# Side sums on the tiles of the main loop: attention and a long convolution on one core

## The chip, the cores and the metric

The kernel runs on one core of a Trainium2 chip. The metric is the device time of one execution in microseconds, and the change is judged by the ratio of the times after and before. TensorE (PE) multiplies matrices into PSUM, which has eight banks of 512 fp32 columns on 128 partitions. ScalarE (ACT) computes the exponentials, VectorE (DVE) everything elementwise; SyncE (SP), ScalarE and GpSimd (POOL) have queues that issue DMAs. Each engine works off its own instructions in order and waits for the others at semaphores.

## The reference

Two independent heads over 2048 positions and 576 channels, concatenated. Everything is fp32.

```python
# A: a diagonal state-space layer, as a long convolution; D = 576 channels, N = 128 states
P = jnp.exp(logdA[:, :, None] * l[None, None, :])           # l = 0..2047
K = jnp.einsum("dn,dnl,dn->dl", Cc, P, dB).real             # one kernel of 2048 taps per channel
y = irfft(rfft(u padded to 4096) * rfft(K padded))[:, :2048] + u * Dskip
# B: attention with 32 query heads of 18 and one head of keys and values
q = (x @ wq).reshape(B, S, 32, 18); k = x @ wk; v = x @ wv  # k, v: 2048 x 18
p = softmax(q k^T * 18 ** -0.5); out = (p v) @ wo
return concatenate([a, b], axis=-1)
```

## The kernel before

**The main loop** is the attention. A *score* is one pair of heads against 128 keys for 512 queries: eight matmuls, each on a tile of 64 rows by 32 columns of the array, fp16, into a two-bank PSUM tile `s` (two such tiles take turns). ScalarE takes the exponential of the whole tile, 128 x 1024, into `P` (ten buffers). A *product* (`ops`) multiplies the exponentials of two scores with the values, fp32, again eight matmuls on 64x32 tiles: the upper 64 rows accumulate into one bank, the lower 64 into another, and VectorE adds the two banks at the end of a group of 16 key blocks (`gather`). A group is four heads, a chunk (`c`) is 512 queries: 4 chunks x 8 groups x 16 key blocks x 2 = 1024 scores and 512 products.

**The side sums** are all other matmuls, put between scores and products: the query projection `q` (five k-steps, two column halves; 4 chunks x 5 units `m`), the output projection `op` (five k-steps, two halves of 288 columns, four row blocks a chunk; the last chunk's in parts as its heads finish), and the convolution, which runs in 12 chunks of 48 channels: `kg` multiplies out the convolution kernel from tables of powers, `hu`, `lu`, `hk`, `lk` are the cosine and sine transforms of the input `u` and of the kernel `kt`, `iy` the inverse. Each is made by

```python
def matmul4(nc, ps, w, x, start=True, stop=True):
    for j in range(0, n, 32):
        nc.tensor.matmul(ps[j:e], w[:, j:e], x, start=start, stop=stop, tile_position=(0, j))
```

or the like: four matmuls on tiles of 128 rows by 32 columns. Attention's side sums and the convolution's have one PSUM bank each (`ps_f["a"]`, `ps_f["c"]`). VectorE empties a bank (`evacuate`, `tensor_copy` and so on) before the next sum goes into it.

**The order** of the three engines PE, ACT and DVE is written out when the program is built. `main` keeps a clock of its own for each engine, with a price for each kind of work, and decides what TensorE does next: a score, a product, or a step of a side sum. Generators wrapped in `Stream` stand for the attention's side work (`side`), its normalisation (`prep`) and two streams of the convolution (`fronts` builds tables and kernel, `backs` transforms and multiplies); they say "p" when they want TensorE, "v" for VectorE. In the clock a change between 64-row and 128-row tiles costs `SWITCH`, so side steps are bunched by `ENTER`, `STAY` and `DRY` in `choose`. `RATE` says how much VectorE work of the convolution may be issued per pair of scores.

**The end.** The kernel `ksb` of a convolution chunk goes through memory to change its layout: `kg`, evacuation, DMA `kd`, four DMAs `kt`, then `hk`/`lk`, some 30 elementwise products and sums (`ks`, `acc`, `sv`, `w`), `iy`, the addition to `u`, and the DMA `outa`. When the scores are done, `drain` finishes the convolution and `finish` the output projection of the last chunk.

Of the kernel before, what the change touches and what calls it, by code (L numbers as in the profile page):

```python
# [47 lines left out]
RATE = 1.9  # L48
# [6 lines left out]
DRY = 1.0  # L55
ENTER = 0.7
EDGE = 0.25
STAY = 0.4
# [18 lines left out]
class Clock:  # L77


    def __init__(self):  # L80
        self.t = self.v = self.a = 0.0
        self.work = self.side = 0.0
        self.last = ""
        self.tiling = 0
        self.s = [0.0] * NS
        self.fill = {"a": 0.0, "c": 0.0}

    def tile(self, rows):

        if rows != self.tiling:  # L90
            self.tiling, self.t = rows, self.t + SWITCH

    def pe(self, cost, *after):
        self.tile(128)
        self.t = max(self.t, *after) + cost if after else self.t + cost
        self.side += cost

    def main(self, cost, *after):
        self.tile(64)
        self.t = max(self.t, *after) + cost  # L100
# [5 lines left out]
    def filled(self, bank):  # L106

        self.fill[bank] = self.v + 0.25
# [45 lines left out]
class Stream:  # L154


    def __init__(self, gen, clock, bank, ahead=AHEAD):
        self.gen, self.k, self.bank, self.ahead = gen, clock, bank, ahead
        self.kind, self.ready, self.holds = "v", 0.0, False
        self.live, self.asked, self.work = True, -1, 0.0  # L160

    def advance(self):
        w0 = self.k.work
        r = next(self.gen, None)
        self.work += self.k.work - w0
        if r is None:
# [4 lines left out]
    def at(self):  # L171

        if not self.live or self.kind != "p":
            return 1e9
        return self.ready if self.holds else max(self.ready, self.k.fill[self.bank])

    def event(self):

        if not self.live or self.kind in "wbp":
# [3 lines left out]
    def go(self, step):  # L183

        k = self.k
        if not self.live or self.kind in "bp":
# [11 lines left out]
def matmul4(nc, ps, w, x, start=True, stop=True):  # L198

    n = w.shape[-1]  # L200
    for j in range(0, n, 32):
        e = min(n, j + 32)
        nc.tensor.matmul(ps[j:e], w[:, j:e], x, start=start, stop=stop, tile_position=(0, j))  # L203


class Attention:
# [7 lines left out]
    def __init__(self, tc, ctx, aps, clock):  # L214
# [11 lines left out]
        self.ps_f = {b: pool(f"ps_f{b}", 1, space=PSUM) for b in "ac"}  # L226
# [4 lines left out]
    def bank(self, n, name, bank="a"):  # L231
        self.k.pe(0.0, self.k.fill[bank])
        return self.ps_f[bank].tile([P, CT], F32, tag="f" + bank, name=name)[:, :n]

    def load_x(self, c, pool, **k):
        t = pool.tile([P, 5, CT], F32, name=f"x{c}", **k)
        self.nc.sync.dma_start(t, self.a["xT"][c])
        return t

    def load_wq(self, m):  # L240
        self.nc.sync.dma_start(self.wq[m], self.a["wq"][m, :, :, :MQ[m][1]])

    def setup(self, tp, conv):
# [24 lines left out]
        nc.gpsimd.memset(x0[64:, 4, :], 0.0)  # L268
# [6 lines left out]
        for k in range(5):  # L275
            n = DT[k][1]
            nc.sync.dma_start(x0[:n, k, :], a["xT"][0, :n, k, :])
        nc.scalar.dma_start(self.sel, a["sel"][:, 0:45])
# [1313 lines left out]
```

## Time and profile before

| | |
|---|---|
| median of 3 runs (lowest, highest) | 1172.84 us (1171.32, 1174.79) |
| the profiled execution | 1173.67 us |
| its span, first to last instruction | 1171.9 us |
| busy: PE, ACT, DVE | 1107.6, 1040.0, 1015.0 us |
| mean granted clock of TensorE | 0.991 |

In the rows a group of instructions has the line of the kernel, the engine, the operation and the tiles it writes and reads; `x` is how many. For matmuls "64*32" is the part of the array. An fp32 matmul leaves two records, since it makes two passes, an fp16 one leaves one. A record of a matmul lasts until its modelled end, so back-to-back matmuls overlap: how long TensorE needs for one is seen from start to start. PEld is the weight load, which runs beside the matmuls. "Idle before, releaser" says how long the engine idled before instructions of the group and what ended it.

### The profile page before, as it was taken

Reading aid. Unit: us, or ns where it says so; the run is one execution under the profiler, and the core shown is the slowest. Engines: PE = TensorE matmul, PEld = TensorE weight load, DVE = VectorE, ACT = ScalarE, POOL = GpSimd, SP = SyncE. Lnnn points to the kernel's source line nnn. Section 1 sums busy time; section 2 is a strip of 40 time slices with the busy share of each in tenths; the row PEclk is TensorE's granted clock in tenths of the full one; section 3 lists DMA queues with packets and bytes.
Section 4 is the critical chain, followed back from the end, with each engine's and each line's share of the span. In section 5 each row is a group of like instructions: output and inputs, shape, how many; then the busy total and the mean of one; then the engine's idle time right before and its main releaser. Section 6 shows DMA issues by size and latency. Waiting matters only on the chain.

```text
span 1171.9 us, 53466 instructions
## 1 busy us (share of the span) xinstructions
PE 1107.6 (95%) x24126; PEld 419.0 (36%) x24126; DVE 1015.0 (87%) x1713; ACT 1040.0 (89%) x1052; POOL 141.6 (12%) x257
## 2 busy tenths in 40 slices
PE   6899999999999999999899999999988999999986
PEld 2333333333333333433333333333333333333323
DVE  4868998998998997998899897998789899799583
ACT  3789999998999998999899999888899999999980
POOL 5303310112210100010401100001120000000000
PEclk9999999999999999999999999999999999999998
DMA  7412512113222003131412202113222210302101
GB/s 222 132 49 80 175 29 83 47 44 103 88 69 96 28 32 97 62 112 29 131 47 89 75 25 75 57 40 82 69 68 74 66 36 22 103 30 76 59 21 65
DMA packets 59358, 84.66 MB, mean 72 GB/s; under 512 B 14867, under 2 KB 35335, under 8 KB 58613
## 3 DMA queue, kind: packets, MB, share of 16 engines
q1 hardware_dynamic: 47557, 73.24, 19.5%
q0 software_dynamic: 10848, 7.37, 2.5%
q8 instruction: 190, 3.11, 1.1%
q10 hardware_dynamic: 720, 0.58, 0.2%
q14 instruction: 43, 0.35, 0.1%
HBM read 46.59 MB, written 33.85 MB: 69 GB/s over the span
## 4 chain that ended last, share of the span: by engine, by line
PE 66%; ACT 19%; DVE 7%; issue 4%; DMA 3%; SPq 0%; ACTq 0%; DVEq 0%
PE ops L836 24%; ACT P L538 18%; PE s L527 17%; PE q L418 6%; PE op L203 5%; PE iy L203 3%; PE kg L1260 3%; PE lk L203 2%; PE hk L203 1%; PE lu L203 1%; PE hu L203 1%; DMA xr<-xT 1%; ACT P L536 1%; PE fin L203 1%; DVE t L128 1%
## 5 line engine op out<-in xcount | busy, mean ns | idle before, releaser
L538 ACT ACTIVATE P<-s 128x1024 f32<-128x1024 f32 x992 | 975.8, 1028 | 69.3 <-PE ops L836 17.8
L836 PE MATMUL ops<-P,v_sb 64*32 64x512 f32 x8192 | 539.2, 593 | 1.9 <-DVE u L1050 1.4
L527 PE MATMUL s<-aug,kaug 55*32 55x512 f16 x8192 | 417.6, 383 | 33.1 <-ACT P L538 28.0
L527 PEld LDWEIGHTS <-kaug 55*32 55x32 f16 x8192 | 134.9, 90 | 386.8 <-issue 375.9
L836 PEld LDWEIGHTS ops<-P,v_sb 64*32 64x32 f32 x8192 | 146.9, 106 | 75.8 <-issue 46.0
L468 POOL DMA_DIRECT2D qd<-qh x116 | 66.2, 578 | 412.9 <-DVE qh L136 410.0
L418 PE MATMUL q<-x,wq_sb 128*32 128x256 f32 x1360 | 104.1, 389 | 0.4 <-DVE un L144 0.4
L203 PE MATMUL op<-wo_sb,oT 126*32 126x288 f32 (+1 forms) x1056 | 88.2, 416 | 0.0
L128 DVE TENSOR_TENSOR tab<-tab,tt 128x576 f32<-128x576 f32 (+1 forms) x72 | 59.2, 822 | 2.0
L128 DVE TENSOR_TENSOR tab<-fr,dif 128x576 f32<-128x576 f32 (+1 forms) x72 | 58.7, 815 | 0.0
L128 DVE TENSOR_TENSOR tt<-fr,sum 128x576 f32<-128x576 f32 (+1 forms) x72 | 58.7, 815 | 0.0
L128 DVE TENSOR_TENSOR tab<-sum,fr 128x576 f32<-128x576 f32 (+1 forms) x72 | 58.7, 815 | 0.0
L128 DVE TENSOR_TENSOR tab<-tab 128x576 f32<-128x576 f32 (+1 forms) x72 | 58.6, 814 | 0.0
L418 PEld LDWEIGHTS q<-x,wq_sb 128*32 128x32 f32 x1360 | 29.4, 108 | 71.5 <-issue 64.2
L1171 POOL MEMSET fr<- 128x192 f32 x24 | 9.9, 495 | 371.5 <-DVE tt L128 239.4
L203 PE MATMUL iy<-w,dft_sb 128*32 128x192 f32 x768 | 41.6, 340 | 8.6 <-DVE u L128 8.6
L128 DVE TENSOR_TENSOR acc<-acc,pt 128x1728 f32<-128x1728 f32 (+2 forms) x36 | 48.7, 1354 | 0.7
L128 DVE TENSOR_TENSOR pt<-us,ks 128x1728 f32<-128x1728 f32 (+2 forms) x36 | 48.0, 1351 | 0.3
L536 ACT ACTIVATE P<-s,bias 128x1024 f32<-128x1024 f32 x32 | 32.9, 1124 | 16.6 <-PE s L527 10.6
L132 DVE COPY ksb<-kg 128x192 f32<-128x192 f32 x48 | 17.3, 360 | 33.3 <-PE kg L1260 33.0
L203 PEld LDWEIGHTS op<-wo_sb,oT 126*32 126x32 f32 (+1 forms) x1056 | 22.9, 108 | 60.7 <-issue 50.7
L1260 PEld LDWEIGHTS kg<-tab 128*32 128x32 f32 x2304 | 35.0, 110 | 25.0 <-issue 14.6
(167 smaller groups left out, 1039.5 us busy)
## 6 DMA issues: line engine op xcount, KB each, us to landing
od<-o SPq DMA_DIRECT2D x31, 256.0 KB
aug<-qd SPq DMA_DIRECT2D x124, 55.0 KB
u<-u SPq DMA_DIRECT2D x12, 384.0 KB
kd<-ksb SPq DMA_DIRECT2D x12, 384.0 KB
kt<-kd SPq DMA_DIRECT2D x48, 96.0 KB
outa<-u SPq DMA_DIRECT2D x12, 384.0 KB
pw<-pw SPq DMA_DIRECT2D x8, 528.0 KB
oT<-od SPq DMA_DIRECT2D x16, 252.0 KB
```

The source lines that it names most:

```text
L128: return self.v.tensor_tensor(out, *a, **k)
L132: return self.v.tensor_copy(out, *a, **k)
L203: nc.tensor.matmul(ps[j:e], w[:, j:e], x, start=start, stop=stop, tile_position=(0, j))
L418: nc.tensor.matmul(ps[o, 256 * f:256 * f + 256], w[:, k, i], xt[:, k, x], start=(k == 0), stop=(k == 4), tile_position=(0, 32 * j))
L468: q.dma_start(qd[h:h + n, row + d:row + d + nd, cs], src[i1:i1 + n * nd, :cs.stop - cs.start])
L527: nc.tensor.matmul(ps[e:e + 32, j, :], self.kaug[r, kb * P + e:kb * P + e + 32], t[r, :], start=True, stop=True, tile_position=(64 * j, e))
L536: nc.scalar.activation(pt, ps, AF.Exp, bias=self.bias, scale=SCALE / QQ)
L538: nc.scalar.activation(pt, ps, AF.Exp, scale=SCALE / QQ)
L836: nc.tensor.matmul(o_ps[32 * j:32 * j + 32, b, cs], self.v[r, kb, :], pts[2 * pi + j // 2][r, j % 2, cs], start=(kb == 0), stop=(kb == 15) ...
L1171: nc.gpsimd.memset(t[:, :, 0:NF:8], one)
L1260: nc.tensor.matmul(ps[32 * g:32 * g + 32, d, :], t[:, :32], t[:, 32:], start=(j == 0), stop=(j == 1), tile_position=(0, 32 * g))
```

## The change

All side sums of the loop but three small ones go over to tiles of 64 rows by 32 columns. A sum now has a pair of banks, one for each half of its columns. In the first pass the upper 64 rows of the contraction work for bank 0 and the lower 64 for bank 1; in the second pass they change places. Between the passes stands a drain of TensorE.

```diff
+def halves(nc, ps, cols, w, x, swap, start, stop):
+    for j in range(0, P, 32):
+        for b in range(2):
+            r, i = slice(64 * b, 64 * b + 64), b ^ swap
+            nc.tensor.matmul(ps[j:j + 32, i, cols], w(r, i, j), x(r, i, j), start=start, stop=stop, tile_position=(64 * b, j))
...
-        self.ps_f = {b: pool(f"ps_f{b}", 1, space=PSUM) for b in "ac"}
+        self.ps_f = pool("ps_f", 1, space=PSUM)
...
+    def pair(self, n, name):
+        self.k.pe(0.0, self.k.fill)
+        t = self.ps_f.tile([P, 2, CT], F32, tag="f", name=name)
+        return t[:, :, :n]
+    def flush(self):
+        self.nc.tensor.drain()
+        self.k.pe(0.12)
```

The query projection, whose last k-step has 64 rows of data (laid into both row halves now, by extra loads of x and wq), takes nine steps; the output projection of the first three chunks likewise, with 20 rows a head in a padded layout `wop` of wo (18 rows, two repeated in the other half), for which `normalize` loads the heads with eight DMAs and scales all with one tile of reciprocals. The last chunk loads wo again in the layout of before.

```diff
+        for swap, k in [(0, k) for k in range(5)] + [(1, k) for k in range(4)]:
...
+            if (swap, k) == (1, 0):
+                self.flush()
+            halves(nc, ps, slice(0, n), wi, xi, swap, (swap, k) == (0, 0), (swap, k) == (1, 3))
+            K.pe(0.43 * n / 256)
```

In the convolution `hu` and `lu` become one sum `dtu` in one bank pair (`hk`, `lk`: `dtk`), and the two sums of a `kg` and of an `iy` become one each:

```diff
+            yield "p", max(ready, K.fill), False
+            ps = self.at.pair(2 * NE, f"dt{nm}{j}")
+            for swap, h in ((0, 0), (0, 1), (1, 0), (1, 1)):
+                if (swap, h) == (1, 0):
+                    self.at.flush()
+                halves(nc, ps, slice(h * NE, h * NE + NE), ..., swap, (swap, h) == (0, 0), (swap, h) == (1, 1))
+                K.pe(0.33)
...
+            V.tensor_copy(x, ps[:, :, NE:])
```

Only one side sum is open at a time now (`holder`). The rules that order the work change with it:

```diff
-RATE = 1.9
+RATE = 2.5
...
-DRY = 1.0
-ENTER = 0.7
-EDGE = 0.25
-STAY = 0.4
+DRY = 0.6
+EDGE = 0.3
+URGE = 1.0
+OVER = 0.5
...
-    def tile(self, rows):
-        if rows != self.tiling:
-            self.tiling, self.t = rows, self.t + SWITCH
...
+            if wanted(st) and K.t + 0.45 <= last + (URGE if st is not side and K.v < K.t + DRY else OVER):
                 conv.count(st)
```

What this makes of the order, on TensorE at the first sum of the output projection, first before (`s` is a score, `ops` a product, `op` a step of the sum; a score is eight pairs of LDWEIGHTS and MATMUL):

```order
L836 MATMUL ops_2_7549<-P_5_9_7811,v_sb 32x512 x4
...
L527 MATMUL s_4_11_7864<-aug_113,kaug 32x512
L203 MATMUL op_0_0_7877<-wo_sb,oT_6125 32x288 x4
L527 LDWEIGHTS kaug
...
L836 MATMUL ops_2_7549<-P_5_10_7854,v_sb 32x512 x4
```

and after, where the step has eight matmuls and steps and products stand in no fixed turn:

```order
L878 MATMUL ops_1_7793<-P_3_5_7976,v_sb 32x512 x4
...
L549 MATMUL s_2_7_8074<-aug_113,kaug 32x512
L204 MATMUL op_0_8085<-wo_sb,oT_7064 32x288 x8
L549 LDWEIGHTS kaug
...
L204 MATMUL op_0_8085<-wo_sb,oT_7064 32x288 x16
```

Between two scores now stand one step or two, where before one step was set between two scores and a product between the next two.

TensorE at the end of the loop, before (`iy` is the last chunk's inverse transform, `fin` the closing output sums):

```order
L836 MATMUL ops_7_21960<-P_15_14_22392,v_sb 32x512 x4
L203 MATMUL op_1_1_1_22443<-wo_sb,oT_21134 32x288 x4
L836 MATMUL ops_7_21960<-P_14_15_22413,v_sb 32x512 x4
...
L203 MATMUL iy_22472<-w_22357,dft_sb 32x192 x16
L203 MATMUL iy_22490<-w_22357,dft_sb 32x192 x16
L203 MATMUL fin_22520<-wo_sb,oT_21134 32x288 x16
```

and after (`dtk` is the transform of the kernel, `s_15_15` the last score):

```order
L204 MATMUL kg_1_25735<-tab_1_24701 32x64 x96
...
L549 MATMUL s_15_15_25842<-aug_113,kaug 32x512
...
L878 MATMUL ops_7_25120<-P_15_15_25851,v_sb 32x512 x4
L204 MATMUL dtk_25870<-kt_25835,dft_sb 32x192 x32
L204 MATMUL dtk_25907<-kt_25835,dft_sb 32x192 x32
L204 MATMUL iy_25976<-w_25966,dft_sb 32x192 x64
L196 MATMUL fin_26055<-wo_sb,oT_21778 32x288 x8
```

The last `kg` stood 45 scores before the end and stands ahead of the last score now, with the transform behind the loop.

VectorE at the last kernel of the convolution (`kg` to `ksb`, its transform in `sck`), before:

```order
L132 COPY ksb_20272<-kg_1_1_21595 128x4x16x3
L128 TENSOR_TENSOR oT_21134<-oT_21134,db_0_21450 126x512
L132 COPY part<-op_0_0_0_21663 128x288
L136 TENSOR_SCALAR dn_7_21629<-dn_7_21629 28x128
...
L132 COPY sck_21643<-hk_21811 128x384
L128 TENSOR_TENSOR sck_21643<-lk_21851,sck_21643 128x384
```

and after:

```order
L120 TENSOR_TENSOR us_25354<-us_25354 128x768
L124 COPY ksb_24154<-kg_1_25735 128x4x16x3 x2
L124 COPY sck_25869<-dtk_25870 128x384
L120 TENSOR_TENSOR sck_25869<-dtk_25870,sck_25869 128x384
L120 TENSOR_TENSOR sck_25869<-dtk_25870,sck_25869 128x2x192
```

The work of the last output parts, which stood between the two, is in front of both now.

More of the change, by code (lines that the diff above doesn't have):

```diff
@@ L185, in go @@
         k = self.k
-        if not self.live or self.kind in "bp":
+        if not self.live or self.kind not in "vw":
             return False
@@ L792, in main, with holder @@
         si = pi = part = 0
+        def holder():
+            return next((st for st in [side] + conv.streams if st.holds), None)
         def score():
```

368 lines of the change are left out of this document (191 added, 177 removed).

## The prediction

> **What bounds the kernel now.** I read the page first: busy shares, then the chain that ended last, then the groups.
>
> ```profile
> PE 1107.6 (95%) x24126; PEld 419.0 (36%) x24126; DVE 1015.0 (87%) x1713; ACT 1040.0 (89%) x1052; POOL 141.6 (12%) x257
> PE 66%; ACT 19%; DVE 7%; issue 4%; DMA 3%; SPq 0%; ACTq 0%; DVEq 0%
> L538 ACT ACTIVATE P<-s 128x1024 f32<-128x1024 f32 x992 | 975.8, 1028 | 69.3 <-PE ops L836 17.8
> L527 PE MATMUL s<-aug,kaug 55*32 55x512 f16 x8192 | 417.6, 383 | 33.1 <-ACT P L538 28.0
> ```
>
> The chain is mostly TensorE, and ScalarE idles 69 us waiting, mostly for it; but VectorE and ScalarE are close behind. So the question is what TensorE's work is worth, and what the other two allow. The stretches of the loop (start to first unbiased exponential, 992 scores, tail), from the table by windows:
>
> ```profile
> 25.00:66.00 41.00, 34.44 (x646) 13.55 (x640) 31.88 (x78) 32.17 (x32) 15.35 (x27) 0.92 0.39 112
> 66.00:1135.00 1069.00, 1033.74 (x23009) 389.41 (x22998) 959.85 (x1587) 998.77 (x1010) 114.47 (x205) 1.00 0.22 67
> 1135.00:1172.00 37.00, 22.89 (x348) 10.98 (x340) 15.18 (x30) 2.44 (x4) 0.00 (x0) 0.85 0.15 53
> ```
>
> Columns are PE, PEld, DVE, ACT, POOL busy, clock, DMA share. The middle stretch has 992 of 1024 scores: 1069/992 = 1.078 us a score. VectorE works 960 of it and idles 109. Now the timeline of TensorE; starts (first column) are to be read, not durations, since durations overlap:
>
> ```profile
> 404.47 0.40 PE L527 MATMUL s<-aug,kaug 55*32 55x512 f16 x8
> 404.80 0.69 PE L203 MATMUL op<-wo_sb,oT 126*32 126x288 f32 x8
> 405.42 0.41 PE L527 MATMUL s<-aug,kaug 55*32 55x512 f16 x8
> 405.65 1.04 PE L836 MATMUL ops<-P,v_sb 64*32 64x512 f32 x16
> 406.51 0.40 PE L527 MATMUL s<-aug,kaug 55*32 55x512 f16 x8
> ...
> 408.55 0.40 PE L527 MATMUL s<-aug,kaug 55*32 55x512 f16 x8
> 408.88 0.88 PE L1260 MATMUL kg<-tab 128*32 128x64 f32 x48
> 409.69 0.41 PE L527 MATMUL s<-aug,kaug 55*32 55x512 f16 x8
> 409.91 1.04 PE L836 MATMUL ops<-P,v_sb 64*32 64x512 f32 x16
> ```
>
> From a score (s, 64-row tiles) to a product (ops, 64-row tiles) pass 0.22 us, and a product takes 0.86. From a score to a side sum (128-row tiles) pass 0.33: 0.11 more. A step of the output projection (op, 288 columns) should take 0.86 x 288/512 = 0.48, and the score behind it starts 0.62 later: 0.14 more. So a visit of the side work costs about 0.25 us over its own columns. The built order of before has 445 such visits.
>
> **TensorE before.** Records of the side sums (a step is 8 records: four matmuls, two passes each):
>
> ```profile
> L418 PE MATMUL q<-x,wq_sb 128*32 128x256 f32 x1360 | 104.1, 389 | 0.4 <-DVE un L144 0.4
> L203 PE MATMUL op<-wo_sb,oT 126*32 126x288 f32 (+1 forms) x1056 | 88.2, 416 | 0.0
> L1260 PE MATMUL kg<-tab 128*32 128x64 f32 x2304 | 42.0, 221 | 0.0
> L203 PE MATMUL iy<-w,dft_sb 128*32 128x192 f32 x768 | 41.6, 340 | 8.6 <-DVE u L128 8.6
> L203 PE MATMUL hk<-kt,dft_sb 128*32 128x192 f32 x384 | 20.8, 335 | 0.0
> ```
>
> By columns at the product's pace: q 170 steps x 0.43 = 73; op 132 x 0.48 = 63; the transforms (hk and its three likes, 192 steps, and iy, 96) 288 x 0.32 = 92; kg 288 sets of 64 columns x 0.108 = 31. Side 259; scores 1024 x 0.22 = 225, products 512 x 0.86 = 440; visits 445 x 0.25 = 111. Sum 1035, 1.01 a score against 1.078 that passed. The loop runs 6.6% over its most loaded engine, and that engine is TensorE.
>
> **The change, part by part.** (1) Visits go. The order of after keeps 22 visits with 128-row tiles (the bound's small sums): 6 us instead of 111. (2) The steps: eight matmuls on 64x32 tiles, two row halves into two banks. This is the product's own form, so a step costs its columns, as before. q's last 64 rows are laid into both halves, so nine steps do for ten, and the fifth chunk's steps are 128 wide: 135 x 0.43 + 36 x 0.215 = 66. op in the loop stays 132 steps (three chunks of 36 instead of 40, and all of the last chunk's first three parts, 24, instead of 12), and the end has 12 fewer. Transforms and kg keep their columns. Side 252. (3) kg's sums have 64 columns and now twice the instructions. Ends: no change (0), or the pace of the visit above, (0.81-0.25)/48 = 12 ns a record, is an issue limit and 96 records take 1.12 instead of 0.65: +0.47 x 48 = 23 us. I take 0: the eight matmuls of a score span 0.40 us from first start to last end in the timeline, and one lasts 383 ns on the page, so all eight start within some 25 ns, 3 ns apart; 64-row tiles issue faster than the 6.8 ns a record (0.65 us for 96) that this needs. (4) 127 drains are added. No row shows one. Below, 0; above, the score's 0.41 of which 0.22 is its cadence, 0.19 of tail, and a weight load that can no longer run ahead, 0.11: 0.30. Nearest is what a visit costs on entering or leaving, 0.11 and 0.14, where TensorE also empties; I take 0.15: 19 us (0 to 38). TensorE after: 225+440+252+6+19 = 942, 0.92 a score.
>
> ScalarE: in a stretch with hardly any side work,
>
> ```profile
> 885.45 23.15 ACT L538 ACTIVATE P<-s 128x1024 f32<-128x1024 f32 x25
> L1128 ACT ACTIVATE stage<-stage,hp_sb 128x2112 f32<-128x2112 f32 (+1 forms) x3 | 5.7, 1910 | 0.0
> L1121 ACT ACTIVATE m<-m 128x2112 f32<-128x2112 f32 (+1 forms) x3 | 5.4, 1814 | 0.0
> L1130 ACT ACTIVATE stage<-stage 128x2112 f32<-128x2112 f32 (+1 forms) x3 | 5.4, 1801 | 0.0
> L1128 ACT ACT_TABLE_LOAD x3 | 3.8, 1283 | 0.1
> L538 ACT ACT_TABLE_LOAD x3 | 3.8, 1283 | 0.8 <-PE s L527 0.8
> ```
>
> (23.15-1.03)/24 = 0.92 a score; with the convolution's three bursts of 8 us, (942+24)/1024 = 0.943. It is the floor that TensorE falls to.
>
> VectorE: its instructions stay but for wider evacuations (op 24 copies to 12, iy 24 additions to 12): some 3 us less. What moves is when. The order at the end of the loop, shown above with the change, tells it. The last chunk's kg, 45 scores before the end until now, stands ahead of the last score; its trip through memory, its transform and its products follow the loop, bare. Their prices, on VectorE, SP and TensorE:
>
> ```profile
> 1093.29 0.36 DVE L132 COPY ksb<-kg 128x192 f32<-128x192 f32 x1 [0.43 <-PE kg L1260]
> 1097.91 1.76 SPq L1287 DMA_DIRECT2D kt<-kd  x4
> 1103.09 0.86 PE L203 MATMUL hk<-kt,dft_sb 128*32 128x192 f32 x16
> 1111.46 1.95 DVE L128 TENSOR_TENSOR ks<-sck 128x384 f32<-128x384 f32 x4
> 1136.71 0.95 DVE L128 TENSOR_TENSOR u<-u,dsk 128x768 f32<-128x768 f32 x1
> 1150.83 0.40 DVE L671 TENSOR_TENSOR o_last<-o_last,ops 128x256 f32<-128x256 f32 x1
> ```
>
> kg's evacuation behind other VectorE work 2; evacuated to hk 9.4; two transform sums with evacuation, 3 each, 6; from ks to u 26.2 less 4.0 of interleaved other work, 22; iy 3 and its addition 1; the finish 1171.9-1150.8 = 21, less some 3 for the 12 steps (6 us of TensorE, half of it beside VectorE). Together 62, where now 37 pass. So VectorE's 960 in the loop fall by some 26 to 937 with its saving taken: 0.944 a score.
>
> Loads: the doubled last rows of x and wq, and a second load of wo, go through SP beside other work, and SP issues 12 loads where it issued 10 for the heads of each of the first three chunks, 0.4 us each (four kt loads take 1.76), behind which a score's operands may queue for a microsecond; five are kept ahead, so I count 0. Without that cover the first load's extra piece, 80 KB, delays the first score by under a microsecond, which I count as 0. The one bank pair (before: one bank each for attention and convolution) makes every side sum wait until VectorE has emptied the last; scores and products go in between, so I price this inside the 6.6% below.
>
> **The sum.** Three engines at 0.92, 0.943 and 0.944. I take the 6.6% of now over the highest: 1.006 a score, 998 us. 66 + 998 + 62 = 1126 span, and the 1.8 that the profiled execution had over its span (1173.67 against 1171.9; the median of the runs, 1172.84, is 0.8 below it): 1127.
>
> **Rivals.** (B) Slower: VectorE's idle time stays. Each of 127 sums must end before VectorE can empty the pair, and be emptied before the next begins, and VectorE, in order, may stand in a product first:
>
> ```profile
> PEld iy L203 <- DVE u L128: 11.4, 5, 8.3
> DVE ksb L132 <- PE kg L1260: 33.0, 23, 5.2
> DVE scu L132 <- PE hu L203: 18.5, 11, 2.6
> ```
>
> If it idles 109 again: 66+937+109+62+2 = 1176. It decides at 106 us, 0.83 a sum; my forecast leaves 61. For it: the waits above are of this kind. Against: they arose where sums were starved of slots on TensorE. (C) ScalarE's floor is met: 66+0.943x992+62+2 = 1065; against it, one engine at 1.01 alone ended 6.6% over its work, and now three lie within 3% of each other. (D) A drain costs far more than 0.30: for 1173 the middle stretch would have to take 1043 us, 1.051 a score, TensorE 1.051/1.066 = 0.986, so 1010 us in all and 0.69 a drain; it is also the case in which the change gives back at the drains what it saves at the visits. (E) The change's small sums meet an issue limit of 25 ns a record: kg's 4608 records 115 instead of 31, the transforms' 16 a step 115 instead of 92; TensorE 1049, 1.024 a score, 66+1083+62+2 = 1213. The rows against it: 48 records of kg in 0.56 us, less than half of that, and the eight of a score within 25 ns. The Trainium skill, TensorE: Matmul & The Clock Gate, section "Wait — 56ns, not 53.3ns?", states that no two matmul starts lie under about 25 ns apart; by that rule (E) would be the time, but here tiles side by side start far closer, so the trace disagrees.
>
> **How the numbers follow.** My case 0.64, with its own range 1092 to 1157 (0.97 to 1.035 a score); C, or most of the way to it, 0.10; B 0.16, spread from 1150 to 1195; D 0.08, 1140 to 1190; E 0.02. The range for 8 in 10 leaves out 1 in 10 on each side: 1088 to 1168. No change, within 0.3% (3.5 us, about what three runs can tell), lies where B and D cross 1173: 0.02 of each. Slower: 0.07 of B, 0.02 of D and all of E, 0.11; faster 0.85.
>
> **What would show it.** Starts from score to side step 0.22 instead of 0.33, and from step to score 0.48; the pace of the middle stretch near 1.0 us a score; the span after the last score some 62 us with a bare kd-kt trip; VectorE's idle in the loop near 60. Wrong it is if drains show gaps over 0.3, if kg's sums take more than 1.5 us for 192 records, or if TensorE's waits for VectorE (now 11.4 at most in one group) grow to tens of microseconds.

## The result, and the profile after

| | before | after |
|---|---|---|
| median of the runs (lowest, highest) | 1173.82 us (1171.32, 1178.02) | 1257.03 us (1253.82, 1262.26) |
| profiled execution, its span | 1173.67, 1171.9 us | 1253.82, 1252.0 us |
| loop behind the first 32 scores, a score | 1069 us, 1.079 | 1129 us, 1.139 |
| behind the last score | 36.7 us | 59.2 us |

The ratio of the times is 1.0709 (95% interval 1.066 to 1.0758). The forecast was 1127 us (1088 to 1168): the change made the kernel slower by 83 us where it was expected to save 46. Of the 80 us between the two spans, 60 lie in the loop and 22.5 behind the last score; the start is 2.4 shorter.

The stretches of the loop after, with the columns of the table shown for before (PE, PEld, DVE, ACT, POOL, clock, DMA share, GB/s):

```profile
25.00:63.80 38.80, 32.22 (x716) 14.70 (x715) 33.17 (x80) 32.59 (x32) 17.32 (x31) 1.00 0.41 115
63.80:1192.80 1129.00, 1009.99 (x29817) 548.20 (x29806) 948.14 (x1540) 983.10 (x1010) 114.69 (x205) 0.99 0.21 63
1192.80:1252.00 59.20, 24.89 (x445) 11.27 (x436) 35.83 (x53) 1.68 (x3) 0.00 (x0) 0.71 0.12 42
```

In the middle stretch no engine is fuller than before: TensorE is busy for 1010 of 1129 us, where before it was 1034 of 1069. VectorE idles 181 instead of 109. The page of after says the same, and its chain of waits has a new share, "issue" (time in which an engine waits for nothing that the profile shows), of 10% instead of 4%:

```profile
PE 1082.6 (86%) x31070; PEld 578.4 (46%) x31070; DVE 1023.5 (82%) x1690; ACT 1024.0 (82%) x1052; POOL 141.5 (11%) x256
q8 instruction: 245, 4.01, 1.4%
PE 58%; ACT 25%; issue 10%; DVE 3%; DMA 2%; SPq 0%; POOL 0%; ACTq 0%; DVEq 0%
L560 ACT ACTIVATE P<-s 128x1024 f32<-128x1024 f32 x992 | 959.6, 1033 | 146.3 <-PE s L549 126.0
L204 PE MATMUL kg<-tab 64*32 64x64 f32 x4608 | 61.6, 227 | 30.8 <-issue 28.0
```

Two rows stand out. ScalarE idles 146 us ahead of its exponentials where before it was 69, and 126 of them end with a score. And in front of kg's matmuls TensorE idles 31 us, 28 of them for "issue"; before it idled 0.0 there. TensorE's timeline shows what that looks like:

```profile
411.50 1.07 PE L878 MATMUL ops<-P,v_sb 64*32 64x512 f32 x16
412.36 0.43 PE L549 MATMUL s<-aug,kaug 55*32 55x512 f16 x8
412.58 1.10 PE L204 MATMUL kg<-tab 64*32 64x64 f32 x92
...
414.06 1.01 PE L204 MATMUL kg<-tab 64*32 64x64 f32 x79
417.04 0.35 PE L204 MATMUL kg<-tab 64*32 64x64 f32 x17 [1.97 <-issue]
417.18 0.43 PE L549 MATMUL s<-aug,kaug 55*32 55x512 f16 x8
```

The first 96 records of this sum start within 0.94 us (so do those of most first halves), where the forecast had 0.65. In the second half TensorE stops after 79 records for 1.97 us, and the score behind it comes late. The profile shows no semaphore that it waits for. The trace has one more queue that bears on this, the instruction DMA (the q8 row above: packets, MB, share): 245 packets now,

```profile
q8 instruction: 190, 3.11, 1.1%
```

190 before (the second row). TensorE's records (matmuls and weight loads) are 62,140 after and 48,252 before: 254 to a packet in both, so these packets carry TensorE's program. From here on its instructions are counted by these records. In the stop above the trace has one packet, from 414.13 to 415.57 us, and TensorE goes on 1.47 us after its end. In the middle stretch of after, starts of TensorE's instructions pause for more than 1.05 us 31 times; 24 of these pauses end 1.2 to 1.6 us behind the end of such a packet, with 318 to 503 instructions gone since the packet before it began. Before there are three pauses, none of that kind. So the theory to test became: TensorE outruns the supply of its own instructions.

### The profile page after: what moved, and what is told of

It reads as the page before. It is cut to its first block, busy times and chain, and to the rows that moved or that the text cites. A ratio compares the mean times of both kernels' runs of the same rounds, so it can differ in the third digit from the quotient of the medians.

```text
span 1252.0 us, 67462 instructions
## 1 busy us (share of the span) xinstructions
PE 1082.6 (86%) x31070; PEld 578.4 (46%) x31070; DVE 1023.5 (82%) x1690; ACT 1024.0 (82%) x1052; POOL 141.5 (11%) x256
## 4 chain that ended last, share of the span: by engine, by line
PE 58%; ACT 25%; issue 10%; DVE 3%; DMA 2%; SPq 0%; POOL 0%; ACTq 0%; DVEq 0%
ACT P L560 24%; PE ops L878 21%; PE s L549 13%; PE op L204 5%; PE q L204 5%; PE kg L204 4%; PE dtu L204 3%; PE iy L204 3%; PE dtk L204 3%; DMA xr<-xT 1%; DVE acc L120 1%; ACT P L558 1%; DVE ks L120 0%; DMA raw<-prm 0%; POOL qd L490 0%
## 5 line engine op out<-in xcount | busy, mean ns | idle before, releaser
L549 PE MATMUL s<-aug,kaug 55*32 55x512 f16 x8192 | 464.7, 382 | 60.3 <-ACT P L560 50.0
L549 PEld LDWEIGHTS <-kaug 55*32 55x32 f16 x8192 | 182.2, 91 | 318.5 <-issue 289.4
L204 PE MATMUL q<-x,wq_sb 64*32 64x256 f32 (+1 forms) x2736 | 93.3, 355 | 6.3 <-issue 4.2
L204 PE MATMUL op<-wo_sb,oT 64*32 64x288 f32 (+1 forms) x2112 | 91.2, 404 | 3.2 <-issue 1.1
L204 PE MATMUL kg<-tab 64*32 64x64 f32 x4608 | 61.6, 227 | 30.8 <-issue 28.0
L204 PEld LDWEIGHTS kg<-tab 64*32 64x32 f32 x4608 | 53.9, 106 | 48.1 <-issue 43.7
L204 PEld LDWEIGHTS q<-x,wq_sb 64*32 64x32 f32 x2736 | 52.2, 106 | 29.2 <-issue 15.7
L204 PE MATMUL iy<-w,dft_sb 64*32 64x192 f32 x1536 | 42.6, 335 | 24.0 <-DVE w L120 22.4
L204 PEld LDWEIGHTS op<-wo_sb,oT 64*32 64x32 f32 (+1 forms) x2112 | 43.4, 106 | 31.3 <-issue 17.6
L204 PE MATMUL dtk<-kt,dft_sb 64*32 64x192 f32 x1536 | 50.4, 345 | 8.2 <-DMA kt<-kd 2.9
L204 PE MATMUL dtu<-u,dft_sb 64*32 64x192 f32 x1536 | 50.3, 332 | 8.2 <-DVE scu L120 3.3
```

Source lines behind the costliest of these rows:

```text
L204: nc.tensor.matmul(ps[j:j + 32, i, cols], w(r, i, j), x(r, i, j), start=start, stop=stop, tile_position=(64 * b, j))
L549: nc.tensor.matmul(ps[e:e + 32, j, :], self.kaug[r, kb * P + e:kb * P + e + 32], t[r, :], start=True, stop=True, tile_position=(64 * j, e))
```

## The experiments

The theories of the first four runs: F, the supply of instructions holds kg up, and the scores behind it; D, the drains cost far more than the 0.15 us of the forecast; P, the single pair of banks ties TensorE to VectorE. Diffs are against the changed kernel unless another is named. "Pace" is the loop from score 33 to the last, a score; "stops" are pauses over 0.7 us, from start to start, within one kind of sum.

**1. kg alone on wide tiles again** (one pass, one instruction for two, no drain in it; the builder's clock books 0.25 us more for the change of tiles):

```diff
-                    halves(nc, ps, slice(64 * d, 64 * d + 64), ..., swap, ...)
+                    for g in range(4):
+                        t = self.tab[:, x, g * TB + q * n + d, :]
+                        nc.tensor.matmul(ps[32 * g:32 * g + 32, q, 64 * d:64 * d + 64], t[:, :32], t[:, 32:],
+                                         start=(x == 0), stop=(x == 1), tile_position=(0, 32 * g))
```

> Changed kernel, but the convolution's kg sums alone are back on 128-row tiles: 48 matmuls a sum instead of 96, no drain between halves (103 drains instead of 127), 43 more visits with 128-row tiles. Theory F (TensorE runs out of fetched instructions: a kg sum is 384 TensorE instructions, and in the changed kernel's trace 15 of 24 kg sums stop for 1.2 to 5.4 us in the middle of their matmuls): the stops go, 24 x 2.3 = 55 us less, 43 x 0.25 = 11 more for the visits: about 1210 us, gaps inside kg near 0. Theory D (drains cost the loop its 60 us, 0.47 each): 24 x 0.47 = 11 less and 11 more: 1255. Theory P (the single bank pair makes TensorE and VectorE wait for each other): the pair stays, 1255.

1194.53 us, ratio 1.0189 (1.014 to 1.0238). The pace is 1.073, the stops in kg are gone, VectorE idles 122, and 103 drains and the one pair are still there. 62 of the 83 us hang on kg's form, more than the 47 or so that F had expected; D and P fall as the main cause. Behind the last score 65.6 us pass. The row of kg's group, and the middle stretch and the end by windows:

```profile
L1300 PE MATMUL kg<-tab 128*32 128x64 f32 x2304 | 41.7, 223 | 1.4 <-DVE scu L120 1.0 <-DVE ql L132 0.4
```

```profile
63.70:1126.80 1063.10, 981.64 (x27360) 510.89 (x27345) 940.68 (x1532) 982.05 (x1010) 115.11 (x205) 0.99 0.22 67
1126.80:1192.40 65.60, 26.11 (x588) 13.19 (x587) 40.84 (x62) 2.57 (x4) 0.00 (x0) 0.73 0.11 38
```

**2. kg spread out**: the same instructions in six pieces, with a score or a product between.

```diff
+                K.pe(0.665 / n)
+                if (swap, d) != (1, n - 1):
+                    yield "g", 0.0, True
-            K.pe(0.665)
```

> Changed kernel, but a kg sum is cut into six pieces of 16 matmuls, and between two pieces stands at least one score or product. Same instructions, same drains, same pair. The convolution falls back by this: two whole kg sums stand behind the last score, so the total is no test (the tail should grow from 59 to some 110 us); the pace of the loop is. F: 64 instructions at a time never empty the store, the stops inside kg go and the pace falls from 1.139 us a score to 1.09 or less. D and P: the pace stays at 1.139 or rises, since drains and pair are as before.

1274.62 us, ratio 1.0856 (1.0827 to 1.0886), but of that 108.8 us behind the last score: kg is done too late. In the loop the stops in kg fall from 31 to 8 us and the pace to 1.107, not to the 1.09 that F had expected. Density counts, and spreading does not take all of it away.

**3. Prices that fit better in the builder's clock**, so that only the order moves:

```diff
-        self.k.pe(0.12)
+        self.k.pe(0.3)
...
-            K.pe(0.665)
+            K.pe(0.665 + 2.0 * swap)
```

> Changed kernel with two prices of the scheduler's clock set to what the trace shows: a drain 0.30 us instead of 0.12, the second half of a kg sum 2.0 us more. No instruction is added or removed, only the order moves: the last kg stands 38 scores before the end instead of 1, and no transform is left behind the last score. If the tail is what the prediction made of it (a bare trip through memory, transform and products, 62 of which 59 were measured), it falls back to some 37: about 22 us less. The stops and drains themselves stay under F and D, but scores are put in time around them: up to 15 us less in the loop. Together 1220 to 1235. Under P the loop stays and only the tail goes: 1235.

1219.96 us, ratio 1.0405 (1.0368 to 1.0442). Behind the last score 24.7 us instead of 59.2; the pace hardly moves (1.133) and kg's stops stay (29 us). So what passes behind the last score hangs on the order, and the stops do not.

**4. 151 drains more**, one ahead of every side sum:

```diff
         t = self.ps_f.tile([P, 2, CT], F32, tag="f", name=name)
+        self.nc.tensor.drain()
         return t[:, :, :n]
```

> Changed kernel with one more drain of TensorE ahead of every side sum (151 more, 278 instead of 127), order otherwise the same. It measures a drain. D (0.47 each in the loop): 60 to 70 us more. F with drains at the 0.30 that the gaps show (0.24 to 0.32 behind each): where TensorE is the late engine it counts in full, 151 x 0.30 = 45, elsewhere nothing: 20 to 45 us more, 1275 to 1300. P: nothing.

1313.86 us, ratio 1.1212 (1.1168 to 1.1256): 57 us for 151, 0.38 each, here. That is more than the 20 to 45 us that F had expected, and just under D's 60 to 70: drains are dear in this kernel, but run 1 keeps 103 of them and loses 62 us.

**5. Instructions without the shape.** Run 1 shows that kg's form counts, not whether it is the number of instructions or the 64-row tiles with their exchange. So the kernel of run 1, with each of kg's wide matmuls cut into two of 32 columns:

```diff
-                for x in range(2):
+                for h, x in ((0, 0), (0, 1), (1, 0), (1, 1)):
                     for g in range(4):
                         t = self.tab[:, x, g * TB + q * n + d, :]
-                        nc.tensor.matmul(ps[..., q, 64 * d:64 * d + 64], t[:, :32], t[:, 32:], ...)
+                        nc.tensor.matmul(ps[..., q, 64 * d + 32 * h:64 * d + 32 * h + 32], t[:, :32], t[:, 32 + 32 * h:64 + 32 * h], ...)
```

> The kernel of the first experiment (kg's sums on 128-row tiles, everything else as changed) with each of kg's matmuls cut into two of 32 columns. kg then issues as many TensorE instructions as in the changed kernel (4608 weight loads and 4608 matmuls, where the first experiment has 2304 and 2304), over the same columns, on wide tiles, with no drain and no exchange of banks. Theory F (what stops kg is the supply of instructions, so their number and their density count): stops named issue inside kg come back, 20 to 35 us in the kg rows, the pace of the middle stretch goes from 1.073 towards the changed kernel's 1.139, time 1225 to 1260. Theory S (the shape counts: tiles of 64 rows, whose two halves write two banks and change places, are what stops kg): kg's rows stay under 3 us of stops, time 1188 to 1205.

1254.4 us, ratio 1.0702 (1.067 to 1.0734), the time of the changed kernel, with the same number of TensorE's instructions and no 64-row tile in kg. The row of kg's group on its page, and TensorE's timeline at one sum:

```profile
L1300 PE MATMUL kg<-tab 128*32 128x32 f32 x4608 | 52.7, 199 | 29.1 <-issue 27.6
```

```profile
604.48 1.03 PE L1300 MATMUL kg<-tab 128*32 128x32 f32 x96
605.44 0.41 PE L549 MATMUL s<-aug,kaug 55*32 55x512 f16 x8
605.78 0.95 PE L1300 MATMUL kg<-tab 128*32 128x32 f32 x86
609.37 0.31 PE L1300 MATMUL kg<-tab 128*32 128x32 f32 x10 [2.65 <-issue]
```

The same stop in the same place. So 4,608 more instructions in dense bursts cost 60 us, whatever the tile; 52 of them lie in the loop, whose pace goes from 1.073 to 1.126.

The two traces also show where TensorE stops. Number the packets, and count TensorE's records from the start up to the end of each of the 24 pauses named above. The counts lie on one straight line, 255.3 records more for each packet, and none is more than 5 records off it. Run 5 has 24 such pauses too, on a line of 255.4, none more than 4 off. TensorE stops, then, exactly where the instructions of the packets so far are used up. All pauses over 0.5 us on these lines, as far behind a packet, come to 55 us after and 54 in run 5; in run 1 some 9 us remain. The supply has a pace of its own: in the middle stretch of no kernel here do two packets start less than 3.2 us apart, which makes at most 80 instructions a microsecond, and in the changed kernel a packet starts when TensorE has 266 instructions or fewer left. Ahead of the pauses TensorE starts some 130 (after) to 150 (run 5) a microsecond over 2 us. This settles theory F.

**6. and 7. kg wide, and the end put right by the order.** Both are the kernel of run 1; in 6 a ready step of the convolution goes first unless a projection is due, in 7 a score is booked dearer:

```diff
-        self.k.pe(0.12)
+        self.k.pe(0.38)
...
-            if side.at() <= K.t and (not cs or self.due < self.step + 8 or self.late()):
+            if side.at() <= K.t and (not cs or self.due < self.step + 4):
```

```diff
-        self.k.pe(0.12)
+        self.k.pe(0.38)
...
-        K.main(0.22, K.s[i % NS])
+        K.main(0.25, K.s[i % NS])
```

> The kernel of the first experiment with another order: a flush is booked at 0.38 us instead of 0.12, and a ready step of the convolution goes ahead of a ready step of the projections unless a projection is due within four scores. The last kg's sum then starts 22 scores before the last score instead of behind the projections at the end, and only the inverse transform follows the last score. By theory F with the tail as a matter of order: the pace stays at 1.073 (1064 us for 992 scores), 64 stands ahead, and behind the last score 35 to 45 instead of 65.7: 1165 to 1177, at or a little under the kernel before (1173). If instead the convolution's delay only moves into the loop, the pace rises by what the tail loses, and the time stays at 1185 to 1197.

> The kernel of the first experiment with prices alone changed: a flush booked at 0.38 us instead of 0.12, a score at 0.25 instead of 0.22, so that the order expects slower scores and starts the side work earlier beside them. The last kg's sum starts 14 scores before the last score. By theory F with the tail as a matter of order: pace 1.073, behind the last score 42 to 52 instead of 65.7, time 1172 to 1184. If the convolution's delay only moves into the loop: 1185 to 1197.

6: 1174.18 us, ratio 1.0007 (0.9991 to 1.0022). 7: 1182.19 us, 1.0071 (1.0047 to 1.0094), pace 1.082, 48.1 behind the last score. The middle stretch and the end of 6:

```profile
66.70:1134.00 1067.30, 984.70 (x27640) 509.62 (x27632) 952.09 (x1556) 982.78 (x1010) 115.54 (x205) 0.99 0.22 68
1134.00:1172.40 38.40, 18.06 (x308) 8.18 (x292) 27.52 (x37) 2.20 (x4) 0.00 (x0) 0.81 0.12 43
```

6 is a tie: kg wide, the end as before, all visits gone but some 70, and the pace is 1.077, as in the kernel before (1.079). Call it the tie. By the forecast's sum its pace should have been near 1.006. So kg is only one of two errors, and the next runs look for the other: what does the loop wait for?

**8. The other extra instructions**, in the kernel before: its projections and transforms cut into halves of their columns on wide tiles.

```diff
+    n, c, m = w.shape[-1], ps.shape[-1] // 2, x.shape[1] // 2
+    for h in range(2):
+        for j in range(0, n, 32):
+            nc.tensor.matmul(ps[j:e, h * c:h * c + c], w[:, j:e], x[:, h * m:h * m + m], ...)
```

> The kernel before with the matmuls of its projections, transforms and inverse transforms cut into two of half the columns (128, 144 and 96 instead of 256, 288 and 192), on the same 128-row tiles, in the same order, kg as it was. TensorE issues some 9,400 more instructions, about what the change adds outside kg, over the same columns, without drains or exchange. Theory I (the supply of instructions takes time outside kg too, and ate what the visits gave back): stops and late starts appear between steps and scores, the pace of the middle stretch goes from 1.079 to 1.10 or more, time 1195 to 1230. Theory K (only kg's dense bursts outrun the supply): time 1170 to 1185, gaps of over a microsecond remain few.

1179.09 us, ratio 1.0044 (1.0026 to 1.0061): 9,440 instructions more, not in bursts, cost 5.5 us there. A finer sign is how often the eight starts of one score are spread over 0.1 us or more: 4 of 1024 scores in the kernel before, 6 here, 179 after, 65 in the tie, although the tie has no more instructions than this run (57,532 against 57,692). In the tie they come denser: of all stretches of 2 us the densest hundredth starts 104 a microsecond or more, here 84.

**9. The tie without exchange and drains.** Each row half writes its own bank in both passes, which leaves the exchange out of the sums:

```diff
-            nc.tensor.matmul(ps[j:j + 32, i, cols], w(r, i, j), ...)
+            nc.tensor.matmul(ps[j:j + 32, b, cols], w(r, i, j), ...)
...
-        self.nc.tensor.drain()
```

> The kernel of the run with another order (kg wide, 1174 us), in the same order, with the exchange and its drains taken away: each row half writes its own bank in both passes, so the sums come out without the exchange, and no flush is needed. 103 drains go; instructions, columns and waits stay. If the gap behind a drain is paid by the path: 103 x 0.30 to 0.38 = 31 to 39 us less, 1135 to 1145. If TensorE isn't what the loop waits for: 1163 to 1175.

1163.54 us, ratio 0.9918 (0.988 to 0.9956): 10.6 us for 103 drains, 0.10 each, the second expectation: in the tie the loop does not wait for TensorE alone. And 110 scores now start spread out instead of 65; that late instructions took part of what the drains gave back is likely, and not shown.

**10. and 11. A lighter VectorE**, in the tie and in the kernel before: two of the six table operations cut to a small piece, order unchanged.

```diff
-            tt(im, im, re, op=ALU.add)
+            self.nc.vector.tensor_tensor(im[:, 0:1], im[:, 0:1], re[:, 0:1], op=ALU.add)
...
-            tt(re, re, t, op=ALU.subtract)
+            self.nc.vector.tensor_tensor(re[:, 0:1], re[:, 0:1], t[:, 0:1], op=ALU.subtract)
```

> The kernel of the run with another order (kg wide, 1174 us), in the same order, with two of VectorE's table operations (72 instructions each of 0.82 us) cut to a small piece, so that the tables are left unfinished: some 100 us less of VectorE's work in the loop, nothing else. Theory V (with the visits gone VectorE, 0.94 us a score, bounds the loop through the one pair of banks): the pace falls from 1.077 to 1.02 or less, time under 1118. Theory T (TensorE with drains and instruction gaps still bounds it): pace 1.05 or more, time 1145 to 1172.

> The kernel before, in its own order, with the same two table operations of VectorE cut to a small piece (the tables are left unfinished): some 100 us less of VectorE's work. If TensorE alone bounded the loop before, as the prediction has it: the pace stays above 1.06, time 1150 to 1172. If VectorE bounded it as well: the pace falls below 1.04, time under 1130. The difference between this fall and the fall of the run before it says how far the bound moved to VectorE.

VectorE's busy time falls by 88 us in each (to 931.8 and 927.2). The tie: 1169.46 us, ratio 0.9963 (0.9943 to 0.9983). Before: 1172.8, 0.9986 (0.9973 to 1.0). VectorE bounds neither.

**12. and 13. A lighter TensorE**, in the kernel before and in the tie: of the projections' steps three in five (12) and six in nine (13) get a quarter of their columns. 13's cut, 12's is alike:

```diff
+            z = n // 4 if (swap, k) in ((0, 1), (0, 2), (0, 3), (0, 4), (1, 0), (1, 1)) else n
-            halves(nc, ps, slice(0, n), wi, xi, swap, ...)
+            halves(nc, ps, slice(0, z), wi, lambda r, i, j: xi(r, i, j)[:, :z], swap, ...)
```

> The kernel before, in its own order and with all its instructions, with three of every five steps of the projections (q, and op in the loop) cut to a quarter of their columns, so that the projections are not whole: 102 steps of q x 0.32 + 72 of op x 0.36 = 59 us less of TensorE's columns in the loop. If TensorE bounds the loop and it runs 6.6% over it (the rule of the prediction's sum): 63 us less, 1105 to 1118. If the hand-over between scores, exponentials and products sets most of the pace: a third of that or less, 1150 to 1170.

> The kernel of the run with another order (kg wide, 1174 us), in its own order and with all its instructions, with six of every nine steps of q and op cut to a quarter of their columns: (96 + 12) steps of q x 0.32 (the narrow chunk's half of that) + 72 of op x 0.36 = 61 us less of TensorE's columns. If TensorE bounds: 61 to 65 us less, 1109 to 1115. If the hand-over sets the pace: 1150 to 1172. If the steps, now short, come too fast for the supply of instructions: the time falls by less than in the kernel before, and scores start spread out more often.

Before: 1151.92 us, ratio 0.9813 (0.9787 to 0.984), 22.7 us less for 59 of columns, a share of 0.38. The tie: 1166.32, 0.9933 (0.9912 to 0.9954), 8 us for 61, a share of 0.13, and 98 scores spread out instead of 65. This is the second error at its root: before, too, the loop did not give back what TensorE's columns gave.

```profile
63.50:1111.90 1048.40, 988.92 (x23009) 402.17 (x23002) 957.57 (x1587) 984.66 (x1010) 114.43 (x205) 1.00 0.22 69
```

The middle stretch of 12 has TensorE's busy time 45 us down (1033.74 before), but the stretch is only 21 shorter.

**14. and 15. Lighter exponentials**, in the kernel before and in the tie: 14 of 16 exponentials on 896 elements, their products on 448 columns, the rest left out.

```diff
+            w = CT if kb in (0, 15) else CT - 64
-            nc.scalar.activation(pt, ps, AF.Exp, scale=SCALE / QQ)
+            nc.scalar.activation(pt[:, :, :w], ps[:, :, :w], AF.Exp, scale=SCALE / QQ)
```

> The kernel before, in its own order and with all its instructions, with 14 of every 16 exponentials cut from 1024 to 896 elements and the products that read them from 512 to 448 columns (the rest of the scores is left out): 896 x 0.11 = 99 us less of ScalarE's 942, 448 products x 0.86/8 = 48 us less of TensorE's columns, of which by the share that e12 measured (0.38) 18 us count. If ScalarE's cadence with a delay behind it sets the pace: 60 us or more less on top, under 1100. If TensorE is the nearer bound here: 18 to 50 us less in all, 1123 to 1155.

> The kernel of the run with another order (kg wide, 1174 us), in its own order and with all its instructions, with the same cut of exponentials and products: 99 us less of ScalarE's work and 48 of TensorE's columns, of which by the share that e13 measured (0.13) 6 us count. If with the visits gone the loop hangs on ScalarE's cadence and the hand-over to it: 60 to 99 us less on top, 1070 to 1110. If the instructions of TensorE set the pace: under 20 us less, 1155 to 1174.

ScalarE's busy time falls by 77 and 83 us. Before: 1144.71 us, ratio 0.9769 (0.9753 to 0.9785), 28 us less, of which 18 may be the products' columns. The tie: 1152.53, 0.9812 (0.9771 to 0.9853), 22 less, a little more than the second expectation (under 20) and far from the first. No single engine carries the pace.

**16. and 17. The tie with q's sums made as the products are**: matmuls of 512 columns, each row half into its own bank for all columns, no exchange, no drain; VectorE adds the two banks.

```diff
-            halves(nc, ps, slice(0, n), wi, xi, swap, (swap, k) == (0, 0), (swap, k) == (1, 3))
+                    nc.tensor.matmul(ps[j:j + 32, b, z], w[r, k, f:f + 32], xt[r, k, x0 + z.start:x0 + z.stop],
+                                     start=(k == 0), stop=(k == 4), tile_position=(64 * b, j))
...
+        V.tensor_copy(qs[:, :n], ps[:, 0, :])
+        V.tensor_tensor(qs[:, :n], qs[:, :n], ps[:, 1, :], op=ALU.add)
```

> The kernel of the run with another order (kg wide, 1174 us) with q's sums in the form of the products: matmuls of 512 columns, each row half into its own bank, no exchange, no drain, and VectorE adds the two banks (a copy and an addition of 512 columns more per sum, 19 x 1.1 = 21 us of VectorE). The order is rebuilt with a score booked at 0.25 and the limit of the convolution's work at 2.8; the last kg begins 25 scores before the end. 19 drains and about 2,400 TensorE instructions fewer. If drains (0.10 each on the path, as the run without exchange showed) and late instructions (about 20 us in the tie, a quarter of the extra instructions) count: 5 to 8 us less, 1165 to 1171, VectorE's addition costing 1 or 2 of it. If a step of 0.86 us holds scores up, or VectorE's addition comes ahead of other work: 1178 to 1190.

> The same kernel with a score booked at 0.265 and the limit at 2.5: another order, the last kg begins 21 scores before the end. As the run beside it, within 6 us of it: 1165 to 1175 if drains and late instructions count, 1178 to 1190 if the long steps or VectorE's addition hold the scores up.

16: 1166.13 us, ratio 0.9938 (0.9916 to 0.9959). 17: 1171.13, 0.9979 (0.9962 to 0.9996), both in the first range expected. 16 is the fastest whole kernel here. VectorE does 20 us more than in the tie (1039.0 against 1019.3) and TensorE issues 2,432 instructions fewer (55,100); 84 drains are left of 103. Two rows of its page, and its middle stretch:

```profile
PE 1050.2 (90%) x27550; PEld 513.2 (44%) x27550; DVE 1039.0 (89%) x1728; ACT 1020.3 (88%) x1052; POOL 141.8 (12%) x256
q8 instruction: 218, 3.57, 1.3%
```

```profile
64.80:1125.20 1060.40, 983.94 (x26472) 487.07 (x26457) 971.75 (x1594) 978.48 (x1009) 115.14 (x205) 0.99 0.23 68
```

That drains and instructions brought it, and not the rebuilt order, is likely but not shown: 16 and 17 differ by 5 us in the order alone.

## Why the prediction was wrong, step by step

**(1) The visits: right on TensorE, counted too high in time.** From score to step pass 0.22 us, from one step to the score 0.48, as forecast, and two steps take 0.97:

```profile
422.58 0.43 PE L549 MATMUL s<-aug,kaug 55*32 55x512 f16 x8
422.80 0.70 PE L204 MATMUL op<-wo_sb,oT 64*32 64x288 f32 x16
423.28 0.43 PE L549 MATMUL s<-aug,kaug 55*32 55x512 f16 x8
423.50 1.19 PE L204 MATMUL op<-wo_sb,oT 64*32 64x288 f32 x32
424.47 0.43 PE L549 MATMUL s<-aug,kaug 55*32 55x512 f16 x8
...
425.40 1.56 PE L204 MATMUL op<-wo_sb,oT 64*32 64x288 f32 x32
426.75 0.43 PE L549 MATMUL s<-aug,kaug 55*32 55x512 f16 x8
```

The columns of the steps, (2), hold too. But 111 us off TensorE were not 111 us of time.

**(3) kg's doubled instructions at 0: the step that turned the sign.** The forecast chose between 0 and an issue limit per record, and had no term for the supply of instructions. The upper end, 23 us, came from a misread row: the 0.81 us from kg to the score holds the way out of the wide tiles, 0.14, but not the way in, so its 48 records took 0.67, about what their columns cost (0.65), and showed no limit at all. The 0 rested on the eight starts of a score, 3 ns apart. But 96 records of kg take 0.94 us where there is no stop, 9.9 ns each and not 6.8, some 14 us over the forecast for all 48 halves; and on top come the stops. Runs 1 and 5 measure the whole step: 62 and 60 us. In the trace of after the exponentials of scores whose eight starts are spread out come 110 us later in all than ScalarE's usual step of some 0.91 us would have them, 58 of it behind kg's sums and 47 behind products. What could have warned was there before the change: 190 instruction packets of 16 KB on the page, in the trace never less than 3.3 us apart in the loop; and that TensorE executed 41 instructions a microsecond on average, while half a sum of kg would bring 192 in the 0.65 us of the forecast, was computable.

**(4) The drains: 0.15 taken.** On TensorE one costs 0.34 us, the median of the 107 sums of 127 after in which the step with the drain can be set against the same step without it: more than the upper end of 0.30. In the rows above, the two steps from 425.40 hold a drain and take 1.35 instead of 0.97. In time it is 0.10 each where they were taken away (run 9) and 0.38 where they were added to the changed kernel (run 4). The term of 19 us for 127 is bracketed by 13 and 48.

**The sum's rule, 6.6% over the most loaded engine: the other step that failed.** It was read off one kernel and used as a law. The tie has TensorE at 225 + 440 + 252 for the columns, 48 visits of kg and 22 others at 0.25 (17.5) and 103 drains at 0.34 (35), 970 us or 0.947 a score, and runs at 1.077, 14% over it. Runs 10 to 15 say why: per microsecond taken off an engine the time falls by 0.06 or less for VectorE, by 0.38 and 0.13 for TensorE. In both kernels the exponentials start 166 us later in all than one each 0.912 us would (some 20 of it are ScalarE's own work for the convolution). The commonest delay, 0.15 to 0.2 us, comes nearly always on a score that stands behind a product: 344 of 353 times before, 196 of 205 in the tie. Each score waits its turn through TensorE, ScalarE and back. The rule missed by (1.077 - 1.006) x 992 = 70 us, kg by 60: 1127 + 130 = 1257. That the two add up so exactly is chance, since the drains and the small stops are in both.

The tie saves 111 - 17.5 = 93.5 us of visits, of which 0.38 x 93.5 = 36 might have come, by run 12. Against it stand about 11 us of drains (run 9) and some 10 us of stops where the packets are used up. That leaves some 15 us that are not accounted for. What the one pair of banks or the new order takes was not tested alone.

A small error in the sum: VectorE's 960 less 26 is 934, not 937, so ScalarE's 0.943 was the highest term; that moves the forecast by 1 us. VectorE worked 948 us in the loop.

**The tail: right.** 62 us forecast, 59.2 measured, with the bare trip of the last kg through memory and the long wait ahead of the inverse transform. The trip, `kd` to `dtk`, takes 5.1 us where 9.4 were forecast, the way from there to `iy` 30.9 where it was to be 28:

```profile
1193.73 0.34 SPq L1329 DMA_DIRECT2D kd<-ksb  x1
1198.85 0.48 PE L204 MATMUL dtk<-kt,dft_sb 64*32 64x192 f32 x2 [2.50 <-DMA kt<-kd]
1229.76 5.73 PE L204 MATMUL iy<-w,dft_sb 64*32 64x192 f32 x128 [22.40 <-DVE w L120]
```

**The rivals.** B (VectorE's idle time stays) gave 1176 and a slower kernel by a wrong road: VectorE's idle time grew to 181, but with kg's form alone put back it is 122 (run 1), so 59 of it follow from kg; and 88 us less work for VectorE in the tie give back 5 (run 10). C did not come. D wanted 0.69 a drain; it is 0.10 to 0.38. E gave 1213 and had its finger on the right sums, kg's, with 0.02 of the chances; its mechanism, a limit of 25 ns from start to start, is not it: 92 records of kg start within 0.88 us. Of the three signs of being wrong two came: drains over 0.30 us and kg's sums over 1.5. The third, long waits of TensorE for VectorE, shows only in the tail, in the 22.4 us above.

## What to carry to other kernels

Count the instructions that a change adds to the engine with the most of them, and above all how densely they come: a burst of a few hundred small matmuls stopped the engine here for two microseconds, although 96 of their records start within a microsecond. The sign before the change is the instruction queue: how many packets, how close together they come, and how many instructions a microsecond that allows. A slack measured over the busiest engine of one kernel is no law; cut that engine's work by a known amount and see what share of it the time gives back, before pricing a change by the work it removes. Where sums can be made without an exchange and VectorE can add the halves, that form was a little faster here (runs 16 and 17, 1166 and 1171 us against the tie's 1174, in other orders).

## What the runs showed of the hardware

- TensorE's instructions arrive during the run, in packets of 16 KB, one for some 253 of its instructions in four kernels (190 for 48,252, 218 for 55,100, 227 for 57,532, 245 for 62,140), and a packet takes 0.88 to 1.44 us after (5% to 95%; median 1.08). The Trainium skill, Trainium Architecture — The Big Picture, section "The software stack", says that the streams are moved into each engine's memory when the program is loaded, with instructions of 64 bytes; the size agrees with 16,384 / 253 = 64.8, which leaves room for a few instructions without a record; the time does not: the trace has these packets through the whole execution.
- In the loops of all 19 kernels two of these packets never start less than 3.2 us apart, so the supply gives at most some 80 instructions a microsecond; TensorE's starts reach some 130 to 150 over the 2 us ahead of a stop, and 41 on average in the kernel before.
- The stops of more than 1.05 us last up to 5.4 us and end 1.2 to 1.6 us behind a packet's end (24 of 31 pauses after, 24 of 35 in run 5), each within 5 instructions of the point where the packets so far are used up. Why the next packet is not asked for earlier stays open.
- A drain is worth 0.10 us of time in the tie, where drains between the passes were taken away, and 0.38 in the changed kernel, where drains ahead of the sums were added. Between the passes it adds 0.34 us on TensorE in both.
